# Query features of the three kept token blocks: turned by VectorE in pieces of 32 rows and put together in DRAM, in place of TensorE transposes with ScalarE copies

## The chip, the cores and the metric

The kernel runs on one core of a Trainium2 chip. A core has five engines that run their own instruction streams: TensorE (PE in the profile, with its weight loads as PEld), VectorE (DVE), ScalarE (ACT), GpSimd (POOL) and SyncE (SP), whose queue issues nearly all DMA transfers here. Sixteen DMA engines move the data. The metric is the device time of one execution in microseconds (us); lower is better.

## The reference

Four layers, alternately A and B, act on x of 2048 tokens by 576 features, all in float32. A is attention of 32 heads of 18 with one shared key and value head. B is linear attention with learned feature maps, and the change lies in B:

```python
phi_q = concat([softmax(q @ w_phi), softmax(-(q @ w_phi))])   # per head: 18 + 18 = 36 features
phi_k = concat([softmax(k @ w_phi), softmax(-(k @ w_phi))])
kv = einsum("bhsf,bhsd->bhfd", phi_k, v);  z = einsum("bhsf->bhf", phi_k)
o  = einsum("bhqf,bhfd->bhqd", phi_q, kv) / (einsum("bhqf,bhf->bhq", phi_q, z) + 1e-6)
x  = x + o.reshape(B, S, D) @ wo        # x is layer-normed before q, k, v
```

The sum over all tokens in kv and z means that no output of B can be made before the keys of the last token are in. The query features of a token (32 heads x 36 = 1152 numbers) can be made earlier, and have to be kept until then.

## The kernel before, in words

The tokens are cut into 16 blocks of 128. The program runs over two layers (`LAYERS = 2`), each one A followed by one B.

*The attention of A* (`attend`) runs block by block in bursts of scores, exponentials on ScalarE and sums. Between the bursts TensorE also does the work of B for blocks whose attention is done: `mix` projects keys, values and queries of a block, adds the keys to the state `kv`, and turns the query features, which lie as tokens x features, into features x tokens. This it does with `block_transpose`: one VectorE instruction turns each 32 x 32 square of the 128 x 1152 tile in place of its square, and four DMAs, one for each 32 tokens, put the squares where they belong in a DRAM tensor, `spill[i]` of 1152 x 128. One such DMA moves 32 features x 36 squares x 32 tokens; a contiguous piece is 32 numbers, 128 bytes.

*The end of the layer.* The last three blocks, `KEPT = 13`, 14 and 15, are done after the attention, in `leave`. There `keys_in` makes the keys and the state (`first_keys`, `second_keys`, `last_keys`) and `queries_in` the query features: `queries` (two halves of 28 matmuls on `wpq`, in the weight place c, each followed by `feature_start`, VectorE and an exponential on ScalarE), `feature_end` for both halves (a sum and a reciprocal on VectorE, the multiply on GpSimd), then `flip_features` and `spill_features`. `flip_features` turns the 1152 features in 11 groups of 108 (the last of 72) by TensorE against an identity, four groups to a PSUM bank, and ScalarE copies them to the tile `phs` (L676, L681). `spill_features` writes it with two DMAs in pieces of 512 bytes (L693, L694). The features of block 13 live in the tile `featk`, those of block 14 in `featq`, those of block 15 in the room `xsc`. The tile `phs` has two buffers. In `leave` TensorE's instructions are chained in the order in which they were traced.

`leave` also fetches weights again: `wob` into place a and, in layer 0, `wq` into place b (L220). `finish_state` lays the state out as `kvb`, and with that the read-out can begin.

*The read-out of B* (`token_tile`, 16 jobs): the features of a block come back from DRAM (`load_features`, L698 and L699, tile `pht`, one buffer for even and one for odd blocks), `read_out` multiplies them with `kvb` (44 matmuls, L804), divides by the sums on VectorE (L811 to L814), turns the result by TensorE (L307, L311), splits it into a high and a low part (ScalarE L132, L313, VectorE L135, L316), projects with `wob` (2 x 14 matmuls, L257) and adds the residual (L321). In layer 0 `next_queries` and `project_queries` follow, which begin the next attention; in layer 1 the block is written to the output.

*The order.* `pipelined` advances the jobs in rounds. In each round one more job starts, and each started job runs to its next `yield STAGE`; then the late jobs get their turn, among them `flips(leave())`. `leave()` runs whole before the first round. When it returns, block 13 is done, block 15 has both halves of its projection, block 14 only the first. `flips` does the rest in spread-out rounds: after one round the second half of block 14's projection; three rounds later its `feature_end`, transposes and spill; two rounds later those of block 15. `advance(job, n)` counts negative yields, which stand for TensorE work. The rounds give the order of tracing; a scheduler then sets the order on each engine, earlier traced work first where it is ready by its own estimate of times. The SP queue and each engine work in the order so fixed, and an instruction that waits holds up those behind it.

Of the kernel before, what the change touches and what calls it, by code (L numbers as in the profile page):

```python
# [62 lines left out]
def kernel(ctx, tc, x_in, wq, wk, wv, wo, wqkv, w_phi, wob, out):  # L63
# [209 lines left out]
    def run(gen):  # L273
        for _ in gen:
            pass
# [390 lines left out]
                feature_end(e, 0, V)  # L666
            yield from project(po, st["wpq"], b * HALF, xs, lambda: feature_start(heads(po), e, b, copies))

    def flip_features(e, pht, ps, copies):
        phi = e.rearrange("p h s d -> p (h s d)")  # L670
        for g0 in (0, 4, 8):
            g1 = min(g0 + 4, NKG)
            pt = ps.tile([P, 4, P], F32, name="ps")
            for g in range(g0, g1):
                m = 2 * DH * (KG if g < NKG - 1 else H - KG * (NKG - 1))
                T.transpose(pt[:m, g - g0, :], phi[:, g * 6 * DH : g * 6 * DH + m], idf)  # L676
            g2 = min(g1, NKG - 1)
            parts = [(slice(0, 6 * DH), g0, g2)] + ([(slice(0, 4 * DH), NKG - 1, NKG)] if g1 == NKG else [])
            for rows, ga, gb in parts:
                if copies is A:  # L680
                    A.activation(pht[rows, ga:gb, :], pt[rows, ga - g0 : gb - g0, :], AF.Copy)  # L681
                else:
                    V.tensor_copy(pht[rows, ga:gb, :], pt[rows, ga - g0 : gb - g0, :])
            yield -440
        return pht

    def feature_rows(spill, i):
        full = 6 * DH * (NKG - 1)
        return (spill[i, :full, :].rearrange("(g r) t -> r g t", r=6 * DH), spill[i, full:, :])

    def spill_features(pht, spill, i):
        rows, rest = feature_rows(spill, i)
        nc.sync.dma_start(rows, pht[: 6 * DH, : NKG - 1, :])  # L693
        nc.sync.dma_start(rest, pht[: 4 * DH, NKG - 1, :])  # L694

    def load_features(pht, spill, i):
        rows, rest = feature_rows(spill, i)
# [3 lines left out]
    def block_transpose(blocks, src, dst, pause=0):  # L701
        V.transpose(blocks, src)
        for _ in range(pause):
            yield
        for q in range(P // 32):
            rows = slice(q * 32, (q + 1) * 32)
            nc.sync.dma_start(dst[:, rows].rearrange("(b f) t -> f b t", f=32),
                              blocks[rows, :].rearrange("f (b t) -> f b t", t=32))
            yield
# [41 lines left out]
    def queries_in(i, xs, eq, st, ps, spill):  # L751
        yield from queries(xs, eq, st, ps, A)
        for b in range(2):
            feature_end(eq, b, G)
        pht = st["sp"].tile([P, NKG, P], F32, name="phs", bufs=2)
        yield from flip_features(eq, pht, ps, A)
        spill_features(pht, spill, i)

    def advance(job, count=1):
        while count:  # L760
            v = next(job, DONE)
            if v is DONE:
                return
            count -= v is not STAGE and not isinstance(v, Kind) and v < 0
# [514 lines left out]
    for layer in range(LAYERS):  # L1279
# [194 lines left out]
        with psx, tc.tile_pool(name=f"s{layer + 1}", bufs=2) as sp:  # L1474
            if not last:
                reload_w4(sp)

            def leave():
                xn = layer_norm(c, stats, sp, A, "xo")
                advance(second_keys)  # L1480
                xl = sp.tile([P, 9, P], F32R, name="xs3")
                advance(transposed(xn, xl, ps, A, LOE), 2)
                queued = [queries_in(i, x, feature_room(name), st, ps, spills[layer])
                          for i, x, name in ((KEPT, kept, "featk"), (c - 1, xs, "featq"))]
                advance(queued[0])
                both = sp.tile([P, 9, PW], F32R, name="xsc").bitcast(F32).rearrange("p a b -> p (a b)")
                ek, eq = (both[:, k * 2 * D : (k + 1) * 2 * D].rearrange("p (h s d) -> p h s d", s=2, d=DH)
                          for k in range(2))
                last_keys = keys_in(c, xl, ek, st, ps)
                queued.append(queries_in(c, xl, eq, st, ps, spills[layer]))  # L1490
                advance(last_keys, 2)
                run(load("wob", "a", wob, slice(0, D), engines=(A, V)))
                advance(last_keys, 2)
                if not last:
                    run(load("wq", "b", wq, slice(0, D), engines=(A, G)))
                advance(queued[0])
                advance(last_keys)
                advance(queued[2])
                run(finish_state(st, sp, ps))
                advance(queued[2])  # L1500
                advance(queued[1])
                run(queued[0])
                before = None
                for i in traced(nc)[mark:]:
                    if i.engine == mybir.EngineType.PE:
                        if before is not None:
                            tc.add_manual_dep(i, before, NOSYNC, reason="order")
                        before = i.name
                return queued[1:]

            def flips(queued):
                for rounds, job, count in ((1, 0, 1), (3, 0, 3), (2, 1, 3)):
                    for _ in range(rounds):
                        yield STAGE
                    advance(queued[job], count)
                for job in queued:
                    run(job)

            def room(i):
                if i % 2:  # L1520
                    return sp.tile([P, NKG, P], F32, name="pht", bufs=1)
                return bw.tile([P, NKG, P], F32, name="pht")

            def token_tile(i):
                pht = room(i)
                load_features(pht, spills[layer], i)
                if i not in left:
                    xres[i] = sp.tile([P, D], F32, name="xt", bufs=6)
                    nc.sync.dma_start(xres[i], xd[i])
                yield STAGE  # L1530
                yield STAGE
                yield from read_out(i, pht, st, sp, ps)
                if last:
                    nc.sync.dma_start(out[i * P : (i + 1) * P, :], xres[i])
                else:
                    nc.sync.dma_start(xd[i], xres[i])
                    yield STAGE
                    yield from next_queries(i, None, layer + 1, st, bw, sp, ps)

            order = range(NT)  # L1540
            st["sp"] = sp
            jobs = [token_tile(i) for i in order]
            for job in jobs[:2]:
                next(job)
            st["late"].append(flips(leave()))
            if last:
                run(pipelined(jobs, st["late"]))
            else:
                settle(layer + 1, ps, jobs)
# [27 lines left out]
```

## Time and profile before

| | |
|---|---|
| three runs | 2676.86, 2673.14, 2677.76 us (median 2676.86) |
| the profiled execution | 2676.42 us, span of the trace 2674.6 us |
| mean granted TensorE clock | 0.991 |
| L676: transposes of the three blocks, TensorE | 66 in the run, 33 in each layer |
| L681: their copies, ScalarE | 24 in the run, 9.1 us |
| L693, L694: their spills, SP | 6 + 6 issues |
| L702 on `pht<-featq`: the same turn for the other 13 blocks, VectorE | 26 in the run, 35.8 us |
| L707 on `phi<-pht`: their spills, SP | 104 issues |

The end of layer 0 (from the last scores of its attention to the first of the next) lies at about 1216 to 1452 us of the span, that of layer 1 at 2525 to 2675. Times in the profile's rows are from the span's start. A row of the instructions in order of time reads: start us, length us, engine, line, operation, output<-input, shapes, count, and in brackets the idle time of the engine before it with what ended that. A row of stretches reads: start:end, length, then busy us of PE, PEld, DVE, ACT and POOL, each with its number of instructions, the granted TensorE clock, the mean busy share of the 16 DMA engines, and GB/s. A row of groups ends with busy us, mean ns of one, and idle time before them with its causes. SPq is SP's queue: the time there is that of issuing. TensorE's matmuls overlap, so the lengths of neighbouring rows can sum to more than the time between their starts.

### The profile page before, as it was taken

The page shows a single profiled execution, that of the slowest core. Times are in us where ns is not written, and L with a number is a line of the kernel's source. Part 1 is how long each engine was busy: PE and PEld are TensorE (multiplying, and loading weights), DVE is VectorE, ACT ScalarE, POOL GpSimd, SP SyncE. Part 2 cuts the span into 40 slices and gives each one's busy share as a digit, 9 for nine tenths or more (in the row PEclk, how much of TensorE's full clock was granted, in tenths as well). Part 3 has the DMA queues.
Part 4 walks back from the last instruction along what each step waited for, and adds up shares of the span by engine and source line. Part 5 has one row for each costly group of instructions (what it writes and reads, how often), then busy time and mean ns, then how long its engine had stood idle before and what let it go on. Part 6 is the DMA issues. An engine that isn't in the chain of part 4 may idle for free. (4 is left out here: it accounts for less than half of the span.)

```text
span 2674.6 us, 55524 instructions
## 1 busy us (share of the span) xinstructions
PE 2602.2 (97%) x22002; PEld 1442.2 (54%) x22002; DVE 1265.0 (47%) x2871; ACT 2153.8 (81%) x2529; POOL 66.0 (2%) x106
## 2 busy tenths in 40 slices
PE   7989999999999999999999999999999999999999
PEld 6633454445444444438996344444444444444498
DVE  8435354444444444436774424444444444444265
ACT  4588889989999999994334999999999999999821
POOL 1000000000000000002000000000000000000010
PEclk9999999999999999999999999999999999999999
DMA  5466243222222222225643312222222222222164
GB/s 182 144 146 171 70 127 100 59 53 60 60 59 57 55 57 57 59 66 158 188 152 105 105 51 59 60 60 60 59 60 59 60 60 57 56 55 55 48 196 140
DMA packets 491634, 232.97 MB, mean 87 GB/s; under 512 B 237734, under 2 KB 458214, under 8 KB 491366
## 3 DMA queue, kind: packets, MB, share of 16 engines
q1 hardware_dynamic: 489894, 226.37, 31.4%
q8 instruction: 177, 2.90, 0.5%
q10 hardware_dynamic: 1472, 2.95, 0.4%
q14 instruction: 91, 0.75, 0.1%
HBM read 130.62 MB, written 96.67 MB: 85 GB/s over the span
## 5 line engine op out<-in xcount | busy, mean ns | idle before, releaser
L1047 ACT ACTIVATE pt<-sc 128x1024 f32<-128x1024 f32 x2036 | 1923.4, 1054 | 180.4 <-PE sc L574 160.3
L574 PE MATMUL sc<-qst,kst 56*128 56x512 f32 x3840 | 698.6, 452 | 21.0 <-ACT pt L1047 20.6
L574 PEld LDWEIGHTS sc<-qst,kst 56*128 56x128 f32 x3840 | 319.4, 185 | 561.7 <-ACT pt L1047 511.8
L853 PE MATMUL acc<-pt,vst 128*32 128x512 f32 x4096 | 499.8, 600 | 0.1
L853 PE MATMUL ps<-pt,vst 128*32 128x512 f32 x4048 | 486.7, 604 | 6.1 <-DVE featq L607 3.2
L853 PEld LDWEIGHTS ps<-pt,vst 128*32 128x32 f32 x4048 | 109.8, 110 | 234.0 <-issue 226.1
L853 PEld LDWEIGHTS acc<-pt,vst 128*32 128x32 f32 x4096 | 104.6, 109 | 211.7 <-issue 209.2
L321 DVE TENSOR_TENSOR xc<-xc,acc 128x288 f32<-128x288 f32 x60 | 27.3, 455 | 349.5 <-PE acc L257 349.5
L257 PE MATMUL ps<-wahi,xs 128*128 128x288 f32 x702 | 152.5, 304 | 2.5 <-ACT xs L132 1.9
L257 PE MATMUL ps<-wchi,xs 128*128 128x288 f32 x576 | 127.2, 307 | 0.0
L257 PE MATMUL acc<-wdhi,on 128*128 128x288 f32 x540 | 120.6, 309 | 3.3 <-DMA on<-od 3.3
L257 PEld LDWEIGHTS ps<-wahi,xs 128*128 128x128 f32 x702 | 116.1, 190 | 7.1 <-ACT xs L132 2.6
L257 PE MATMUL ps<-walo,xs 128*128 128x288 f32 x390 | 114.9, 297 | 0.0
L452 PE MATMUL ps<-xsc,wbhi 128*128 128x256 f32 x576 | 107.3, 285 | 0.6 <-ACT xsc L132 0.6
L474 ACT ACTIVATE pc<-ps 128x256 fp32r<-128x256 f32 x80 | 30.4, 384 | 94.0 <-PE ps L452 92.5
L257 PEld LDWEIGHTS ps<-wchi,xs 128*128 128x128 f32 x576 | 94.1, 188 | 19.0 <-issue 18.1
L607 DVE COPY featk<-acc 128x288 f32<-128x288 f32 x50 | 22.8, 457 | 172.0 <-PE acc L257 172.0
L132 ACT ACTIVATE xs<-ps 128x512 fp32r<-128x512 f32 x36 | 21.4, 595 | 102.6 <-PE ps L307 102.6
L257 PEld LDWEIGHTS acc<-wdhi,on 128*128 128x128 f32 x540 | 88.8, 189 | 25.0 <-issue 23.6
L257 PE MATMUL acc<-wahi,xs 128*128 128x288 f32 x450 | 100.0, 308 | 0.5
L257 PE MATMUL ps<-wclo,xs 128*128 128x288 f32 x320 | 94.3, 295 | 0.0
L452 PEld LDWEIGHTS ps<-xsc,wbhi 128*128 128x128 f32 x576 | 91.2, 192 | 1.6 <-ACT xsc L132 1.1
(261 smaller groups left out, 3062.3 us busy)
## 6 DMA issues: line engine op xcount, KB each, us to landing
qst<-qd SPq DMA_DIRECT2D x360, 72.0 KB
od<-parts SPq DMA_DIRECT2D x512, 36.0 KB
pht<-phi SPq DMA_DIRECT2D x32, 540.0 KB
qd<-pc SPq DMA_DIRECT2D x64, 256.0 KB
on<-od SPq DMA_DIRECT2D x60, 256.0 KB
phi<-pht SPq DMA_DIRECT2D x104, 144.0 KB
xd<-xc SPq DMA_DIRECT2D x33, 288.0 KB
flipped<-pht SPq DMA_DIRECT2D x112, 72.0 KB
```

The costliest lines, as they stand in the source:

```text
L132: A.activation(dst_hi, src, AF.Copy)
L257: T.matmul(dst, xs[:, slot, :], w[half][:, k, c0 : c0 + HALF], start=(n == 0), stop=(n == last))
L321: V.tensor_add(xr, xr, po)
L452: T.matmul(po, lhs, xsc[:, slot, :], start=(n == 0), stop=(n == LASTP))
L474: A.activation(pc[:, 0, :], po, AF.Copy)
L574: T.matmul(sc, kst[head_rows(h), t * P : (t + 1) * P], q[head_rows(h), h // 2, :], start=True, stop=True)
L607: V.tensor_copy(e[:, hs, 0, :], src)
L853: T.matmul(acc[32 * j : 32 * j + 32, :], vst[:, t, :], pts[j], start=first, stop=last)
L1047: A.activation(pt, sc, AF.Exp, scale=SCALE)
```

## The change

`queries_in` takes the way of the other blocks: after `feature_end` one VectorE instruction turns the 128 x 1152 features square by square into a tile of the tag `phs` (128 x 1152 in place of 128 x 11 x 128, still two buffers), and four DMAs write it to the same DRAM tensor in the same layout. `load_features` and all that reads are as before. `flip_features` and `spill_features` go. `flips` waits one round and then runs block 14 to its end (second half of the projection, `feature_end`, turn, spill) and block 15 after it. In `leave`, block 13 runs to its end at the same place as before.

```diff
-    def flip_features(e, pht, ps, copies):
-        phi = e.rearrange("p h s d -> p (h s d)")
-        for g0 in (0, 4, 8):
-            g1 = min(g0 + 4, NKG)
-            pt = ps.tile([P, 4, P], F32, name="ps")
-            for g in range(g0, g1):
-                m = 2 * DH * (KG if g < NKG - 1 else H - KG * (NKG - 1))
-                T.transpose(pt[:m, g - g0, :], phi[:, g * 6 * DH : g * 6 * DH + m], idf)
...
-                    A.activation(pht[rows, ga:gb, :], pt[rows, ga - g0 : gb - g0, :], AF.Copy)
...
-            yield -440
-        return pht
...
-    def spill_features(pht, spill, i):
-        rows, rest = feature_rows(spill, i)
-        nc.sync.dma_start(rows, pht[: 6 * DH, : NKG - 1, :])
-        nc.sync.dma_start(rest, pht[: 4 * DH, NKG - 1, :])
...
         yield from queries(xs, eq, st, ps, A)
         for b in range(2):
             feature_end(eq, b, G)
-        pht = st["sp"].tile([P, NKG, P], F32, name="phs", bufs=2)
-        yield from flip_features(eq, pht, ps, A)
-        spill_features(pht, spill, i)
+        blocks = st["sp"].tile([P, 2 * D], F32, name="phs", bufs=2)
+        run(block_transpose(blocks, eq.rearrange("p h s d -> p (h s d)"), spill[i]))
+        yield STAGE
...
             def flips(queued):
-                for rounds, job, count in ((1, 0, 1), (3, 0, 3), (2, 1, 3)):
-                    for _ in range(rounds):
-                        yield STAGE
-                    advance(queued[job], count)
+                yield STAGE
                 for job in queued:
                     run(job)
```

The function that it now calls, unchanged:

```python
def block_transpose(blocks, src, dst, pause=0):
    V.transpose(blocks, src)
    for _ in range(pause):
        yield
    for q in range(P // 32):
        rows = slice(q * 32, (q + 1) * 32)
        nc.sync.dma_start(dst[:, rows].rearrange("(b f) t -> f b t", f=32),
                          blocks[rows, :].rearrange("f (b t) -> f b t", t=32))
        yield
```

More of the change, by code (lines that the diff above doesn't have):

```diff
@@ L667, in queries @@
             yield from project(po, st["wpq"], b * HALF, xs, lambda: feature_start(heads(po), e, b, copies))
-    def flip_features(e, pht, ps, copies):
-        phi = e.rearrange("p h s d -> p (h s d)")
-        for g0 in (0, 4, 8):
-            g1 = min(g0 + 4, NKG)
-            pt = ps.tile([P, 4, P], F32, name="ps")
-            for g in range(g0, g1):
-                m = 2 * DH * (KG if g < NKG - 1 else H - KG * (NKG - 1))
[L676 to L683, printed above, removed]
-            yield -440
-        return pht
     def feature_rows(spill, i):
```

## The prediction

> **What bounds the kernel now.** I read the page first, then the work by stretches, then the chain of waits and the instructions in order of time around the removed lines. The first line below is the page's share of engines. The next two are stretches: the ends of the two layers, where the changed code runs (start:end, length, busy us of each engine with its instructions, TensorE clock, DMA share, GB/s).
>
> ```profile
> PE 2602.2 (97%) x22002; PEld 1442.2 (54%) x22002; DVE 1265.0 (47%) x2871; ACT 2153.8 (81%) x2529; POOL 66.0 (2%) x106
> ...
> 1216.00:1452.00 236.00, 229.83 (x2481) 219.26 (x2473) 170.86 (x513) 80.42 (x187) 25.17 (x34) 0.99 0.54 166
> 2525.00:2675.00 150.00, 144.12 (x1775) 137.23 (x1769) 93.79 (x267) 31.09 (x72) 15.07 (x14) 0.99 0.50 154
> ```
>
> In these stretches PE is busy 97% and 96% of the time, ScalarE (ACT) 34% and 21%. So a microsecond taken from PE counts, one taken from ScalarE hardly does, and VectorE (72% and 63%) is next. In the chain that ended last, the removed transposes of layer 1 stand as three pieces (start, us):
>
> ```profile
> 2568.37 1.20 PE ps L676 x11
> ...
> 2586.53 1.34 PE ps L676 x11
> ...
> 2595.75 1.34 PE ps L676 x11
> ```
>
> Together 3.88 us. For layer 0 I take the distance from each group's start to the next PE work, from the instructions in order of time:
>
> ```profile
> 1258.80 1.36 PE L676 MATMUL ps<-idf,featk 128*108 128x128 f32 x11
> 1260.23 1.48 PE L804 MATMUL ps<-kvb,pht 108*64 108x57 f32 x44
> ...
> 1280.19 1.15 PEld L676 LDWEIGHTS ps<-idf,featq 128*108 128x108 f32 x11
> ...
> 1281.34 0.47 PEld L307 LDWEIGHTS ps<-idf,xn 128*128 128x128 f32 x4
> ...
> 1290.69 1.15 PEld L676 LDWEIGHTS ps<-idf,xsc 128*108 128x108 f32 x11
> ...
> 1291.83 0.19 PEld L257 LDWEIGHTS ps<-wahi,xs 128*128 128x128 f32 x1
> ```
>
> That is 1.43 + 1.15 + 1.14 = 3.72 us. The whole prize is 3.88 + 3.72 = 7.60 us, 0.28% of the run, if nothing else ends later.
>
> But one place of layer 0 is not bound by PE. Token tile 2 waits for its features from DRAM; the rows are PE's first read-out of tile 2 with the idle time before it, the SyncE (SP) queue ahead of that load, and stretches around it:
>
> ```profile
> 1262.32 1.54 SPq L220 DMA_DIRECT2D wblo<-wqd  x1
> 1263.97 0.34 SPq L693 DMA_DIRECT2D phi<-phs  x1
> 1264.40 1.99 SPq L694 DMA_DIRECT2D phi<-phs  x1
> 1266.49 0.85 SPq L698 DMA_DIRECT2D pht<-phi  x1
> 1267.39 2.59 SPq L699 DMA_DIRECT2D pht<-phi  x1
> ...
> 1273.69 0.29 PE L804 MATMUL ps<-kvb,pht 108*64 108x57 f32 x2 [1.55 <-DMA pht<-phi]
> ...
> 1272.00:1274.00 2.00, 0.45 (x5) 0.28 (x3) 1.94 (x8) 0.00 (x0) 0.84 (x1) 0.97 0.77 217
> 1274.00:1276.00 2.00, 2.00 (x9) 2.00 (x9) 1.26 (x2) 0.00 (x0) 1.95 (x3) 0.50 0.64 189
> 1276.00:1278.00 2.00, 2.00 (x12) 2.00 (x12) 0.77 (x2) 1.12 (x2) 0.00 (x0) 0.68 0.10 15
> ...
> 1262.00:1272.00 10.00, 9.06 (x100) 8.35 (x98) 9.19 (x26) 2.32 (x5) 2.33 (x2) 1.00 0.93 301
> 2572.00:2582.00 10.00, 9.06 (x106) 8.22 (x104) 9.02 (x27) 2.32 (x5) 3.50 (x3) 1.00 0.63 191
> ```
>
> The DMA engines are 93% busy there (reload of wq, then the spill of block 13, then tile 2's features), so the load's landing at 1273.7 is set by what lies ahead of it in the queue, and PE idles 1.55 us. The stall also costs speed: the granted clock is 0.97, 0.50 and 0.68 in three 2-us stretches, which is 2 x (0.03 + 0.50 + 0.32) = 1.7 us of full-speed PE. In layer 1 the DMA share at the same point is 0.63 and no such wait stands.
>
> The rule of the Trainium skill, page "TensorE: Matmul & The Clock Gate", part "The HAM clock gate", is that the clock halves after an idle window of about 3.4 us and recovers after as long a busy one. The trace shows the halving after a shorter idle time, so by the row any stall of 1.5 us may cost another 1.7 us, by the rule only one that fills a window; the sum below needs neither, since this stall stays and no new one is forecast.
>
> **The change part by part.** Removed in each layer: 33 transposes on PE (3.72 and 3.88 us) and 12 copies on ScalarE. PE waited for those copies only this much in the whole run (us, times; from the groups of the read-out's weight loads):
>
> ```profile
> L804 PEld LDWEIGHTS ps<-kvb,pht 108*64 108x64 f32 (+1 forms) x1408 | 44.1, 138 | 7.4 <-issue 6.1 <-ACT phs L681 0.5 <-PE ps L307 0.3
> ```
>
> These 0.5 us lie inside the distances above. Otherwise the copies count as nothing: ScalarE's idle time in these stages hides them.
>
> Added: six VectorE transposes and 24 DMA issues in place of 12. Both are in the trace, because the other 13 blocks of each layer go that way already (groups of instructions; issues with shortest/median/longest ns; a spill of the attention stage, the last thing issued before the stretch that follows; POOL's second multiply of block 13):
>
> ```profile
> L702 DVE STREAM_TRANSPOSE pht<-featq 128x1152 f32<-128x1152 f32 x26 | 35.8, 1377 | 0.8
> ...
> L707 SPq DMA_DIRECT2D phi<-pht x104: 307/587/1825, 343.1 to 2477.2; - x104
> ...
> 1166.13 2.54 SPq L707 DMA_DIRECT2D phi<-pht  x3
> ...
> 1168.00:1170.00 2.00, 1.58 (x14) 0.57 (x16) 0.00 (x0) 2.00 (x4) 0.00 (x0) 1.00 1.15 190
> ...
> 2566.42 1.17 POOL L621 TENSOR_TENSOR featk<-featk,fz 128x576 f32<-128x576 f32 x1 [4.11 <-DVE fz L620]
> ```
>
> VectorE gets 3 x 1.377 = 4.13 us per layer. The spill keeps its 1152 x 128 x 4 = 589,824 bytes, but in 4608 pieces of 128 bytes rather than 1152 of 512. At 190 GB/s it fills the engines for 589,824 / 190e3 = 3.1 us, against 589,824 / 301e3 = 2.0 us at the mixed rate of 1262 to 1272: 1.1 us more each. On SP four issues of 0.59 us make 2.3 us, as L693 and L694 took (0.34 + 1.99); at the longest, 1.8 each, 7.3 us.
>
> Waits that are new: a VectorE transpose stands behind POOL's second multiply of its block (1.17 us), the third also behind the landing of block 13's spill, whose buffer it takes (two buffers). What is queued behind it on VectorE are the splits and divisions of the token tiles (L135, L811 to L814) and the residual adds (L321), and PE's projections (L257) wait for those splits. On SP, the loads of the next tiles' features and residuals queue behind the spills. Moved: all features of blocks 14 and 15 are traced in the second round rather than up to the seventh, so their reductions, multiplies and spills come forward, into 1266 to 1280 and 2575 to 2588.
>
> *Layer 1.* PE gains 3.88. VectorE has this much room and these waits (its busy time is in the third number after the length):
>
> ```profile
> 2568.00:2570.00 2.00, 1.98 (x28) 1.75 (x28) 1.78 (x5) 1.75 (x4) 0.00 (x0) 1.00 0.21 22
> 2570.00:2572.00 2.00, 2.00 (x44) 1.95 (x41) 1.26 (x7) 0.92 (x3) 0.00 (x0) 1.00 0.40 102
> ...
> 2580.67 0.69 DVE L135 TENSOR_TENSOR xs<-ps,xs 128x512 fp32r<-128x512 f32 x1 [0.41 <-ACT xs L132]
> ...
> 2583.80 0.46 DVE L321 TENSOR_TENSOR xt<-xt,ps 128x288 f32<-128x288 f32 x1 [0.94 <-PE ps L257]
> ```
>
> From 2568 to 2582 its idle time is 0.22 + 0.74 + 0.98 = 1.94 us (the last from 9.02 busy in ten). So 4.13 - 1.94 = 2.2 us of its work runs late at 2582, just where tile 1's split (2580.67) is what PE waits for; after 2583.8 it idles again and catches up. Between 0 (the order puts the transposes behind the splits) and 4.13 (all exposed) I take 2.2. The spill's extra DMA time I cost at 0 here, covered by the free 37% of the DMA engines (3.7 us in those ten); without that cover it is 1.1. Layer 1: -3.88 + 2.2 = -1.7.
>
> *Layer 0.* The first group's 1.43 us is gained ahead of the wait for tile 2, so it only lengthens that wait: 0. The load of tile 2 now stands behind a spill that takes 1.1 us longer: +1.1 (between 0, if the spill gets ahead of the wq reload, which VectorE's earlier finish allows, and 5.0, SP's 7.3 less 2.3). The other two groups come after the wait: -1.15 - 1.14 = -2.29. VectorE's extra 4.13 us I cost at 0: PE waits for the DMA until about 1274.8 whatever VectorE does, and the added work ends by then; without that cover it costs up to 2.2 as in layer 1. Layer 0: -1.2.
>
> Sum: -1.7 - 1.2 = -2.9. The profiled execution took 2676.42 us around its span of 2674.6, 0.4 under the median of the three runs (2676.86), so no correction is due: **2673.5 us**. About 0.2% (5.4 us) is what a measurement of this kernel can tell from no change, and this is less.
>
> **The rivals.**
> - *All of it hidden (0.22).* VectorE's transposes fall in its gaps and tile 2's features land no later: -3.88 - 2.29 - 1.43 = -7.6, 2668.8. For it: the DMA falls to 0.10 busy at 1276, VectorE is idle again after 2583. Against: VectorE is 92% and 90% busy just where the work is put.
> - *VectorE becomes the bound (0.20).* Its transposes, traced ahead of the tiles' splits, are taken first in both layers: 2 x 4.13 of exposed time and 1.1 of DMA against 7.6: +1.8, 2678.2. For it: PE already waits at 2580.69 for one split. Against: in layer 0 PE waits for a DMA then.
> - *The loads queue behind the spills: slower (0.10).* All three spills of a layer get onto SP ahead of tile 2's features: 3 x 3.1 instead of 2.0, so these land 7.3 us later. Layer 0: 7.3 - 2.29 = +5.0. Layer 1: the load was issued by 2574.2 (below); with the 3.7 us that it took from issue to use in layer 0 (1269.98 to 1273.69) it lands at 2577.9, then at 2585.2. PE wants it at 2581.4 less 1.2: 5.0 us of stall and 1.7 of clock against 3.88: +2.8. Together +7.8, 2684.2. It decides from about 6 us of lateness in both layers. For it: SP is first come, first served and the spills are now traced before tile 2's load. Against: that load is free to go as soon as tile 0 is read out, before block 14's second half is even projected.
>
> ```profile
> 2573.28 0.92 SPq L699 DMA_DIRECT2D pht<-phi  x1
> ...
> 2581.41 0.56 PE L804 MATMUL ps<-kvb,pht 108*64 108x57 f32 x10
> ```
>
> The Trainium skill speaks for this rival: "DMA: Bandwidth & Descriptors", section Specifications, asks for pieces of at least 512 bytes, and "VectorE: DVE Perf Modes", section "Rules for kernel authors", sends a 128 x 128 transpose to TensorE. By the first, the trace agrees (190 against 301 GB/s); no row here shows the second.
> - *The change does not do what it says (0.03).* PE's freed slots refill with waits one for one: 2676.4.
>
> **How the numbers follow.** The forecast has 0.45; its own range is 2670.2 (VectorE's and the spill's costs at 0) to 2675.5 (VectorE's at 4.13). Faster by over 0.2%: the hidden case and the lower edge of the forecast, 0.22 + 0.05 = 0.27. Slower: the queue rival and the upper edge of the VectorE one, 0.10 + 0.02 = 0.12. Within: 0.61. The range 2667.5 to 2681 takes in the hidden case and the VectorE one and leaves out most of the queue rival.
>
> **What would show it.** Right: no L676 or L681; L702 on phs six times at 1.38 us; PE's wait for tile 2's features in layer 0 above 3 us, landing near 1275; in layer 1 a PE wait of 1 to 2 us on an L135 split; the end of layer 0 earlier by about 1 us and of layer 1 by about 2 more. Wrong: tile 2's load landing before 1273 in layer 0 (the hidden case), PE waits on splits above 3 us in both layers (VectorE), or waits on pht in layer 1 and for tile 3 (the queue).

## The result

The change made the kernel slower: 2703.98 us median of five runs (2702.12 to 2709.11) against 2674.34 for the kernel before beside it, ratio 1.0110, 95% interval 1.0096 to 1.0125. That is 30 us worse, outside the predicted range (2667.5 to 2681), and on the side of the rival "the loads queue behind the spills", though almost four times as dear as that rival was priced (+7.8).

The profiled execution of the changed kernel took 2703.98 us with a span of 2702.2, 27.6 more than before. To see where they lie I cut both traces at the same instructions: the first copy to `osb` after a layer's attention opens the end of a layer, the first exponential of the next attention (on `wchi`) closes that of layer 0, and the last residual add closes that of layer 1. In the trace of before these stand at 1216.91, 1449.21, 2526.24 and 2671.01; in that of the changed kernel (instructions in order of time) here:

```profile
1214.98 0.60 ACT L885 ACTIVATE osb<-acc 128x512 f32<-128x512 f32 x1 [1.20 <-PE acc L830]
...
1461.26 1.94 ACT L1024 ACTIVATE wchi<-sc 128x1024 f32<-128x1024 f32 x2 [2.85 <-PE sc L574]
...
2538.72 0.60 ACT L885 ACTIVATE osb<-acc 128x512 f32<-128x512 f32 x1 [1.20 <-PE acc L830]
...
2698.31 0.46 DVE L321 TENSOR_TENSOR xc<-xc,ps 128x288 f32<-128x288 f32 x1 [1.14 <-PE ps L257]
```

The end of layer 0 grew from 232.30 to 246.28 us (+13.98), that of layer 1 from 144.77 to 159.59 (+14.82); the attention between them from 1077.03 to 1077.46. So both ends lost about the same. All experiments below are read by these two lengths, since the first mark itself varied from 1210.7 to 1217.6 between profiled runs. Each length is that of one execution. The attention between the two ends, which no run changes, varied from 1075.3 to 1078.8, so a difference of a us or two between two ends may be chance.

The page's engine line and the stretches of the two ends after the change:

```profile
PE 2605.3 (96%) x21936; PEld 1442.9 (53%) x21936; DVE 1272.1 (47%) x2877; ACT 2145.5 (79%) x2505; POOL 66.0 (2%) x106
...
1214.00:1464.00 250.00, 229.54 (x2448) 218.46 (x2440) 174.28 (x516) 76.19 (x175) 25.21 (x34) 0.96 0.53 157
2537.00:2702.00 165.00, 147.48 (x1746) 139.59 (x1738) 97.48 (x270) 27.18 (x60) 15.03 (x14) 0.94 0.49 140
```

TensorE is busy 92% and 89% of the two ends (97% and 96% before), at a clock of 0.96 and 0.94 instead of 0.99: the 66 transposes are gone, and its busy time has still risen by 3.1 us, because it ran slower. VectorE has 3.4 and 3.7 us more.

SP's queue and TensorE's idle times in layer 0 after the change show where:

```profile
1260.94 24.55 SPq L684 DMA_DIRECT2D phi<-phs  x12
1285.59 0.94 SPq L675 DMA_DIRECT2D pht<-phi  x1
...
1258.31 1.48 PE L781 MATMUL ps<-kvb,pht 108*64 108x57 f32 x44 [1.26 <-DMA kvb<-featx]
1270.88 0.64 PE L307 MATMUL ps<-idf,xo 128*128 128x128 f32 x4 [2.50 <-DVE xo L790]
1272.27 0.61 PE L257 MATMUL ps<-wahi,xs 128*128 128x288 f32 x1 [0.27 <-ACT xs L132]
1291.72 2.58 PE L781 MATMUL ps<-kvb,pht 108*64 108x57 f32 x44 [12.82 <-DMA pht<-phi]
```

All twelve spill issues of blocks 13, 14 and 15 (L684) stand on SP ahead of tile 2's load (L675). They occupy the queue for 24.55 us, and the load goes at 1285.59, 70.6 us after the first mark, instead of 1266.49, 49.6 after it. TensorE waits 12.82 us for it (1.55 before). What SP itself waited for in that time (us, times, longest), and the last of VectorE's three turns:

```profile
SPq L684 <- DVE phs L679: 10.3, 1, 10.3
...
SPq L684 <- DVE fz L620: 2.6, 1, 2.6
...
1281.15 1.38 DVE L679 STREAM_TRANSPOSE phs<-xsc 128x1152 f32<-128x1152 f32 x1
```

The third turn, block 15's, starts at 1281.15, though the block's features were multiplied by about 1270.8 (GpSimd's last multiply of `xsc` started at 1269.62 and took 1.16). On VectorE it stands behind the residual adds and statistics of tile 1. No idle time stands right before it, and from 1269 to 1270 the DMA share is down to 0.02 with block 13's spill moved, so by 1281 it is its place in VectorE's order, and no longer its buffer, that makes it late. Ten of the 24.55 us are SP waiting for it, and for most of them the DMA engines have nothing to do. The stretches show that, and the clock:

```profile
1268.00:1271.00 3.00, 0.50 (x4) 0.30 (x4) 2.97 (x9) 0.00 (x0) 2.19 (x2) 1.00 0.54 77
1271.00:1278.00 7.00, 6.70 (x29) 6.18 (x29) 4.03 (x12) 1.89 (x4) 0.54 (x1) 0.53 0.48 71
1278.00:1282.00 4.00, 0.90 (x6) 0.66 (x5) 2.29 (x6) 0.00 (x0) 0.54 (x1) 0.93 0.00 0
1282.00:1291.00 9.00, 0.00 (x0) 0.00 (x0) 0.53 (x1) 0.00 (x0) 0.00 (x0) 0.50 0.72 140
1291.00:1296.00 5.00, 4.28 (x54) 4.08 (x54) 1.87 (x7) 0.62 (x2) 0.00 (x0) 0.57 0.71 232
```

From 1278 to 1282 the DMA share is 0.00; then block 15's spill and the late loads move, with TensorE idle. The granted clock is 0.53 in the seven us after the wait of 2.50 and 0.57 in the five after the wait for tile 2: 7 x 0.47 + (5 x 0.43 less half of the 0.72 us still idle) = 5.1 us of full-speed TensorE, 3.4 more than the 1.7 of before. With the waits (1.26 + 2.50 + 0.27 + 12.82 = 16.85, against 0.31 + 0.64 + 1.55 = 2.50 in the same stretch before) that is 14.35 - 3.72 + 3.4 = 14.0, the 13.98 measured.

Layer 1 after the change (SP's queue, SP's waits, TensorE's idle times, VectorE around the two parts of tile 1's split, stretches):

```profile
2581.41 21.77 SPq L684 DMA_DIRECT2D phi<-phs  x12
2603.29 1.15 SPq L675 DMA_DIRECT2D pht<-phi  x1
...
SPq L684 <- DVE fz L620: 9.9, 1, 9.9
...
2582.84 1.48 PE L781 MATMUL ps<-kvb,pht 108*64 108x57 f32 x44 [2.08 <-DMA kvb<-featx]
...
2594.76 0.37 PE L257 MATMUL ps<-wahi,xs 128*128 128x288 f32 x1 [2.02 <-issue]
...
2610.08 2.58 PE L781 MATMUL ps<-kvb,pht 108*64 108x57 f32 x44 [6.12 <-DMA pht<-phi]
...
2589.12 0.63 DVE L135 TENSOR_TENSOR xs<-ps,xs 128x512 fp32r<-128x512 f32 x1
...
2592.72 1.38 DVE L679 STREAM_TRANSPOSE phs<-featq 128x1152 f32<-128x1152 f32 x1 [0.53 <-POOL featq L621]
2594.36 0.29 DVE L316 TENSOR_TENSOR xs<-ps,xs 64x128 fp32r<-64x128 f32 x1
...
2596.00:2604.00 8.00, 7.36 (x33) 6.75 (x33) 3.79 (x9) 0.77 (x2) 0.00 (x0) 0.59 0.72 106
2604.00:2608.00 4.00, 0.00 (x0) 0.00 (x0) 0.45 (x1) 0.00 (x0) 0.00 (x0) 0.75 0.87 193
2608.00:2616.00 8.00, 5.28 (x75) 4.68 (x77) 2.69 (x9) 0.77 (x2) 0.00 (x0) 0.50 0.73 208
```

The same order on SP, with the load 64.6 us after the mark instead of 46.7; here SP's long wait (9.9) falls on block 14, whose second half is only projected after tile 0's read-out. A second loss is VectorE's: between the two parts of tile 1's split (L135 at 2589.12, L316 at 2594.36) stand block 14's and 15's sums and block 14's turn, and TensorE, which needs the split, starts 0.4 us after its second part does, having waited 2.02 us. The granted clock is then 0.59 and, behind the wait for tile 2, 0.50. Layer 0 has the like: the 2.50 us before 1270.88 are a wait for tile 1's division, which stands on VectorE behind the sums of blocks 14 and 15 and block 14's turn.

### The profile page after: what moved, and what is told of

It is laid out like the page before. It is cut to its first block, busy times and chain, and to the rows that moved or that the text cites. A ratio compares the mean times of both kernels' runs of the same rounds, so it can differ in the third digit from the quotient of the medians.

```text
span 2702.2 us, 55360 instructions
## 1 busy us (share of the span) xinstructions
PE 2605.3 (96%) x21936; PEld 1442.9 (53%) x21936; DVE 1272.1 (47%) x2877; ACT 2145.5 (79%) x2505; POOL 66.0 (2%) x106
```

## The experiments

My theory after these traces: the 29 us are a matter of order. `flips` now traces blocks 14 and 15 whole in its second round, so their spills stand on SP ahead of tile 2's load, and that load waits for features that don't exist yet. Rivals: the pieces of 128 bytes; the turns on VectorE; the missing third buffer of `phs`. The table has the lengths of the two ends in the profiled runs less those of before (232.30 and 144.77), and the ratio of the medians to the kernel before beside them.

| kernel | end of layer 0 | end of layer 1 | ratio (95%) |
|---|---|---|---|
| the change | +13.98 | +14.82 | 1.0110 (1.0096 to 1.0125) |
| three buffers of `phs` | +5.84 | +14.18 | 1.0075 (1.0056 to 1.0094) |
| long pieces | +4.05 | +9.42 | 1.0060 (1.0041 to 1.0079) |
| spills on ScalarE's queue | +3.66 | +10.74 | 1.0062 (1.0045 to 1.0078) |
| three buffers, spills of 14 and 15 later | +2.36 | +6.23 | 1.0034 (1.0020 to 1.0048) |
| rounds as before | +2.50 | +0.49 | 1.0019 (1.0008 to 1.0029) |
| rounds as before, long pieces | +0.58 | +1.77 | 1.0005 (0.9995 to 1.0016) |
| rounds as before, block 15's turn moved | -1.69 | +0.99 | 0.9996 (0.9986 to 1.0005) |
| that, and the state's transposes earlier | -1.89 | -1.18 | 0.9999 (0.9990 to 1.0008) |
| rounds, turn moved, block 13 by TensorE | +0.88 | -1.54 | 1.0000 (0.9991 to 1.0009) |
| rounds, turn moved, a half of block 14 in `leave` | +1.04 | +6.32 | 1.0013 (1.0002 to 1.0025) |
| kernel before with the new `flips` | +5.36 | +8.83 | 1.0058 (1.0041 to 1.0076) |

**Rounds as before.**

```diff
-                yield STAGE
-                for job in queued:
-                    run(job)
+                for rounds, job, count in ((1, 0, 1), (3, 0, 0), (2, 1, 0)):
+                    for _ in range(rounds):
+                        yield STAGE
+                    if count:
+                        advance(queued[job], count)
+                    else:
+                        run(queued[job])
```

> The changed kernel with one thing put back: `flips` spreads its work over rounds as before (after one round the second half of block 14's projection, three rounds later block 14's turn and spill, two later block 15's). The turns by VectorE and the spills in 128-byte pieces stay. Only block 13's four spill issues then stand on SP ahead of tile 2's load; those of block 14 stand behind tile 4's. Theory (the order on SP costs the time): nearly all of the 14.0 us of layer 0 and the 14.8 us of layer 1 goes, and 2668 to 2677 us is left, ratio to the kernel before 0.997 to 1.001. Rival (128-byte pieces are what costs, about 4 us a spill against 2): the same bytes move in the same pieces, so at least 2 us a spill, 12 us in all, stays: 2685 or more. Rival (VectorE's six turns and the waits they put ahead of the tiles' splits): the turns stay, 2685 or more.

Measured: 2677.67 us beside 2672.13, ratio 1.0019. SP in layer 0:

```profile
1260.89 6.30 SPq L684 DMA_DIRECT2D phi<-phs  x4
1267.29 0.75 SPq L675 DMA_DIRECT2D pht<-phi  x1
```

Four issues stand ahead of tile 2's load instead of twelve, and it goes 18 us sooner. 11.5 of 14.0 us and 14.3 of 14.8 go, with every turn and every short piece still in place: both those rivals are out as the main cause. By its ratio the kernel stays above the forecast (0.997 to 1.001), so the turns and spills did not bring the gain they were meant to; the later runs look for it.

**Three buffers of `phs`**, the change otherwise as it is.

```diff
-        blocks = st["sp"].tile([P, 2 * D], F32, name="phs", bufs=2)
+        blocks = st["sp"].tile([P, 2 * D], F32, name="phs", bufs=3)
```

> The changed kernel with three buffers of `phs` in place of two, so that block 15's turn doesn't have to wait for the landing of block 13's spill. The order on SP is the same as in the changed kernel (12 spill issues ahead of tile 2's load); on VectorE block 15's turn stands some 20 instructions earlier. Theory: in layer 0 the turn comes at about 1272 instead of 1281, SP's wait of 10.3 us shrinks to about 2, tile 2's load is issued about 8 us earlier, and 8 to 9 of the 14 us go; in layer 1 the turn was late by 3.3 us, so about 3 of the 14.8 go: 2690 to 2695 us, ratio 1.006 to 1.008. Rival (the missing buffer is the whole cause): 2680 or less. Rival (pieces or bandwidth): no change, 2702 to 2706.

Measured: 2694.39, ratio 1.0075. Layer 0 gave back 8.1 of 14.0, as worked out; layer 1 only 0.6 of 14.8 (3 were expected). SP's queue and TensorE's wait, layer 0, then SP in layer 1:

```profile
1259.87 16.06 SPq L684 DMA_DIRECT2D phi<-phs  x12
...
1282.71 1.90 PE L781 MATMUL ps<-kvb,pht 108*64 108x57 f32 x44 [4.28 <-DMA pht<-phi]
...
2572.05 23.15 SPq L684 DMA_DIRECT2D phi<-phs  x12
```

The third turn now comes at 1269.75 and the twelve issues take 16 us instead of 24.55. In layer 1 they still take 23: there the queue waits for block 14's features, which no buffer makes sooner. The missing buffer is the larger part of layer 0's loss and nearly none of layer 1's. It costs by the order: with three buffers the third turn is built in at an earlier place on VectorE.

**Spills of blocks 14 and 15 later**, with three buffers.

```diff
+        turn = block_transpose(blocks, eq.rearrange("p h s d -> p (h s d)"), spill[i], 1)
+        next(turn)                      # the turn alone
+        later.append(turn)              # its four DMAs
...
+                run(later.pop())        # in leave: block 13's DMAs, as before
...
                 yield STAGE
                 for job in queued:
                     run(job)
+                for rounds in (3, 2):
+                    for _ in range(rounds):
+                        yield STAGE
+                    run(later.pop(0))
```

> The changed kernel with three buffers of `phs`, and with the spills of blocks 14 and 15 alone moved back: their projection, sums, multiplies and turns stay in the second round, and their eight issues are traced three and five rounds later. VectorE's order is that of the run with three buffers but for a few small neighbours; SP has only block 13's four issues ahead of tile 2's load. Theory (the order on SP): in both layers the wait on pht goes, and the end of layer 1, which three buffers left 14.2 us longer than before, comes down to within 3 us of before: 2674 to 2681 us in all, ratio 1.000 to 1.003. Rival (the early projections and turns themselves, which push the tiles' divisions and splits back on VectorE): layer 1 stays 8 us or more longer, 2684 or more.

Measured: 2683.12, ratio 1.0034, between the two forecasts. Only eight DMA issues per layer have moved against the run with three buffers, and the ends fall by another 3.5 and 8.0 us; no wait of TensorE on `pht` over 0.3 us is left at tile 2. So in layer 1 SP's order is worth 8 of the 14.8 us. But 6.2 us stay there, which I had given to the rival only from 8 on. They are VectorE's:

```profile
2575.46 0.62 DVE L135 TENSOR_TENSOR xs<-ps,xs 128x512 fp32r<-128x512 f32 x1
2576.03 0.75 DVE L619 TENSOR_REDUCE fz<-featq 128x32 f32<-128x576 f32 x1
2576.70 0.74 DVE L619 TENSOR_REDUCE fz<-xsc 128x32 f32<-128x576 f32 x1
...
2579.04 1.38 DVE L679 STREAM_TRANSPOSE phs<-featq 128x1152 f32<-128x1152 f32 x1 [0.52 <-POOL featq L621]
...
2580.69 0.29 DVE L316 TENSOR_TENSOR xs<-ps,xs 64x128 fp32r<-64x128 f32 x1
...
2581.08 0.37 PE L257 MATMUL ps<-wahi,xs 128*128 128x288 f32 x1 [2.01 <-issue]
2583.96 1.09 PE L307 MATMUL ps<-idf,xo 128*128 128x128 f32 x4 [2.10 <-DVE den L791]
```

Some 4.6 us of block 14's and 15's work, 1.38 of it the turn and 0.52 a wait for GpSimd, stand between the two halves of one split, and TensorE waits for the second. With the rounds as before this work spreads out and those 6 us go too.

**The kernel before with the new `flips`** (TensorE's transposes, no turn, no short piece).

```diff
-                for rounds, job, count in ((1, 0, 1), (3, 0, 3), (2, 1, 3)):
-                    for _ in range(rounds):
-                        yield STAGE
-                    advance(queued[job], count)
+                yield STAGE
                 for job in queued:
                     run(job)
```

> The kernel before (TensorE transposes, ScalarE copies, two spill issues of 512-byte pieces) with only `flips` changed: block 14 and 15 run to their ends in the second round. All six spill issues of a layer then stand on SP ahead of tile 2's load. Theory (the order on SP): slower than the kernel before, as the load waits for block 15's features, though less than by 27 us, since the copies of block 15 don't wait for a buffer as long and a spill takes 2 us: 2682 to 2698, ratio 1.003 to 1.009, with waits of TensorE on pht in both layers. Rivals (pieces; VectorE's turns): neither is in this kernel, so 2673 to 2677.

Measured: 2689.32, ratio 1.0058, in the forecast band, but not by the mechanism forecast. Tile 2's load stands behind block 13's spill alone (at 1264.61), blocks 14's and 15's spills behind it and ahead of tile 3's. What TensorE waits for, in layer 0:

```profile
1264.33 0.76 PE L676 MATMUL ps<-idf,featq 128*108 128x128 f32 x5 [2.58 <-POOL featq L621]
1267.50 1.52 PE L676 MATMUL ps<-idf,featq 128*108 128x128 f32 x6 [2.41 <-POOL featq L621]
```

That is 5.0 us, and layer 1 has the same two waits (2.58 and 2.40): TensorE's own transposes now come up in its queue before GpSimd has multiplied the features. So with the same `flips` SP's order was built another way here; which spills stand ahead of a load can be read from the built program, not from the diff. So the move of `flips` costs by itself, in either version; which queue pays depends on the version, TensorE here, SP and VectorE in the change.

**Spills on ScalarE's queue**, the change otherwise as it is.

```diff
-            nc.sync.dma_start(dst[:, rows].rearrange("(b f) t -> f b t", f=32),
+            (queue or nc.sync).dma_start(dst[:, rows].rearrange("(b f) t -> f b t", f=32),
...
-        run(block_transpose(blocks, eq.rearrange("p h s d -> p (h s d)"), spill[i]))
+        run(block_transpose(blocks, eq.rearrange("p h s d -> p (h s d)"), spill[i], queue=nc.scalar))
```

> The changed kernel with the 12 spill issues of the kept blocks in each layer on ScalarE's queue instead of SP's; the turns, pieces, bytes and `flips` stay as changed. Tile 2's and 3's loads then stand on SP behind no spill. Theory (head of line on SP): the load of tile 2 goes at about 1266 in layer 0 and 2573 in layer 1, and the two PE waits of 12.8 and 6.1 us go; ScalarE's own work behind the waiting issues (the tiles' copies L132 and L313) may stall instead, so 2672 to 2688, ratio 0.999 to 1.005. Rival (the DMA engines' time for 128-byte pieces): the loads share the engines with the same pieces and land as late: 2698 or more. Rival (VectorE): the turns stand as they were, 2690 or more.

Measured: 2688.12, ratio 1.0062, just above the forecast (up to 2688, ratio 1.005). No wait of TensorE on `pht` at tile 2 is left, though the same short pieces share the same engines. But the stall has gone to the queue that issues now, here in layer 1:

```profile
2579.90 17.04 ACTq L684 DMA_DIRECT2D phi<-phs  x8
2597.04 0.60 ACT L132 ACTIVATE xs<-ps 128x512 fp32r<-128x512 f32 x1 [19.97 <-DMA phi<-phs]
...
2597.69 0.40 PE L257 MATMUL ps<-wahi,xs 128*128 128x288 f32 x1 [3.48 <-ACT xs L132]
```

ScalarE does no arithmetic for 19.97 us; its copy for a tile stands behind eight waiting issues, and TensorE waits 3.48 us for that copy. In layer 0 it waits 4.05 us for one behind block 13's issues. So this part of the loss follows the issues from one queue to the other. Another 3.22 us of waiting in layer 1, before 2580.70, is for VectorE's part of a split, behind the early sums and block 14's turn, which this run leaves as they were.

**Long pieces**, with `flips` as changed and with the rounds as before. The features of blocks 13 to 15 land in another order, so their read-out isn't the reference's; the bytes are the same.

```diff
-            nc.sync.dma_start(dst[:, rows].rearrange("(b f) t -> f b t", f=32), ...)
+            nc.sync.dma_start(spill[i].rearrange("(p a) t -> p (a t)", p=P)[rows, :], blocks[rows, :])
```

> The changed kernel, `flips` as changed, two buffers, with each spill DMA writing 32 pieces of 4608 bytes instead of 1152 of 128 (the same bytes; the features of blocks 13 to 15 land in the order of the tokens, so their read-out multiplies other numbers than the reference's). The built order puts block 15's turn where three buffers put it, so the run to compare with is the one with three buffers (2694.39, ratio 1.0075): same turns, same order on SP in layer 0, only the pieces differ. Theory (SP waits for features that aren't made yet, not for the transfer): SP is done 1 to 2 us sooner in layer 0 and in layer 1 about as much, so 2 to 4 us less than with three buffers: ratio 1.006 to 1.007. Rival (the slow pieces are the price, about 4 us a spill against less than 2): 6 us or more less in layer 0 alone, ratio 1.005 or below.

> The changed kernel with the rounds of `flips` as before (the kernel that came to 2677.67), and with each of the four spill DMAs writing 32 pieces of 4608 bytes instead of 1152 of 128. The same bytes move; the features of blocks 13, 14 and 15 land in the order of the tokens, so the read-out of these three blocks multiplies other numbers than the reference's. Theory: with the order put back the pieces are not on the path; TensorE's waits left there are on kvb (1.69 and 1.34 us) and on xo (3.93 and 2.16), not on pht: 2675 to 2680, within 0.1% of the kernel with rounds and short pieces. Rival (short pieces still cost 1 to 2 us each through the loads that share the engines): 2670 to 2674.

Measured: 2688.07, ratio 1.0060, and 2676.62, ratio 1.0005. In layer 0, where turns and SP's order equal those of the run with three buffers, the long pieces gave 1.8 us (+5.84 to +4.05), and TensorE's wait for tile 2 fell from 4.28 to 2.90: at most a small part, though 1.8 us between two single executions is hardly clear of chance. In layer 1 (4.8) they can't be read alone, since block 14's spill there no longer stands ahead of tile 2's load. With the rounds as before the two intervals (1.0008 to 1.0029 with short pieces, 0.9995 to 1.0016 with long) overlap, so a cost of up to some 4 us is neither shown nor excluded there. What the pieces cost the DMA engines is plainer, in stretches in which SP has only spills under way (128 bytes in the changed kernel; 512 in the kernel before with the new `flips`; 4608 in the changed kernel with long pieces):

```profile
1272.00:1274.00 2.00, 1.73 (x8) 1.73 (x8) 1.80 (x5) 0.39 (x2) 0.00 (x0) 0.50 1.00 149
```

```profile
2588.00:2590.00 2.00, 2.00 (x33) 1.67 (x34) 0.50 (x1) 1.31 (x4) 0.00 (x0) 0.65 0.81 232
```

```profile
1270.00:1272.00 2.00, 1.07 (x5) 0.60 (x5) 1.91 (x7) 0.64 (x2) 0.54 (x1) 0.79 0.98 258
```

A spill of 589,824 bytes is 4.0 us at 149 GB/s, 2.5 at 232 and 2.3 at 258.

**Block 15's turn behind tile 2's division**, rounds as before. With rounds as before TensorE's longest waits left are these (layer 0, layer 1):

```profile
1258.53 1.48 PE L781 MATMUL ps<-kvb,pht 108*64 108x57 f32 x44 [1.69 <-DMA kvb<-featx]
...
1280.25 1.07 PE L307 MATMUL ps<-idf,xo 128*128 128x128 f32 x4 [3.93 <-DVE xo L790]
...
2570.04 1.48 PE L781 MATMUL ps<-kvb,pht 108*64 108x57 f32 x44 [1.34 <-DMA kvb<-featx]
...
2589.43 0.78 PE L307 MATMUL ps<-idf,xo 128*128 128x128 f32 x4 [2.16 <-DVE xo L790]
```

```diff
+                    tc.add_manual_dep(turn, st["xos"][-3], NOSYNC, reason="order")   # tile 2's last copy into xo
```

> The kernel with the rounds of `flips` as before (2677.67), with one instruction moved: block 15's turn on VectorE is made to stand behind the division of tile 2 (the last copy into its xo) instead of right before it; SP's order is the same. If the turn's place on VectorE is what left that kernel 5 us behind, TensorE's waits of 3.93 us (layer 0) and 2.16 us (layer 1) on xo shrink by the turn's 1.3 us and by the wait ahead of it, to under 1.5 together: 2671 to 2674, ratio 0.999 to 1.0005. If it isn't, 2676 to 2679.

Measured: 2673.58, ratio 0.9996: level with the kernel before. The waits on xo are 1.46 and 0.93 instead of 3.93 and 2.16, together 2.39, above the 1.5 forecast; the time is in the forecast. The end of layer 0 is 4.2 us shorter, that of layer 1 0.5 longer. One instruction's place on VectorE held most of what the rounds had left.

**What swallowed the rest.** Three runs on top of that one. The state's transposes earlier, so that `kvb` lands sooner:

```diff
                 advance(last_keys)
-                advance(queued[2])
+                for _ in range(4):
+                    next(queued[2])
                 run(finish_state(st, sp, ps))
+                advance(queued[2])
```

> The kernel with rounds as before and block 15's turn behind tile 2's division (2673.58), with the transposes of the state (`finish_state`) traced after 6 of the 14 products of block 15's first half instead of after all 14, so about 1.0 us earlier on TensorE (8 products of 0.135 us). Theory: TensorE's wait for kvb, 1.26 us in layer 0 and 1.46 in layer 1, is what swallowed the gain of block 13's removed transposes; about 1.0 us of it goes in each layer, unless the transposes of the state now wait for VectorE's last addition to it: 2671 to 2673, ratio 0.998 to 0.9995. If that wait takes its place, no change.

Measured: 2671.26, ratio 0.9999, above the forecast 0.998 to 0.9995. The waits for `kvb` are 0.47 and 0.82 instead of 1.26 and 1.46, and in the profiled run the two ends together are 3.1 us shorter than without the move; the medians don't show it. Block 13 by TensorE as before, the other two by VectorE (`if i == KEPT:` with the old `flip_features` and `spill_features`):

> The kernel with rounds as before and block 15's turn behind tile 2's division (2673.58), with block 13 turned by TensorE again (11 transposes, three ScalarE copies, two spill issues of 512-byte pieces); blocks 14 and 15 stay with VectorE. Theory: the 1.2 to 1.4 us of TensorE that block 13's group takes in each layer lie under the wait for kvb (1.26 and 1.46 us), which then shows in no row; so the time is that of the kernel without them, 2672 to 2675, and removing this group was worth nothing. Rival (the group was on the path, as the prediction had it for layer 1): 1 to 3 us slower, 2675 to 2677.

Measured: 2671.97, ratio 1.0000. No wait for `kvb` is left in either layer; the 11 transposes stand in its place. The ratio differs from the run without them by 0.04%, less than either interval is wide. The profiled ends go opposite ways (+2.6 and -2.5 against that run). So it is as the theory has it within what can be told: that group covered a wait. And the second half of block 14's projection moved ahead of the first read-out, in place of the state's move:

```diff
-                advance(queued[1])
+                advance(queued[1], 2)
```

> As the run before in this call (block 15's turn behind tile 2's division), with the second half of block 14's projection moved from the second round into `leave`, ahead of the first read-out. The removed transposes of block 13 stood just ahead of that read-out and covered the landing of kvb; without them TensorE waits 1.69 and 1.34 us for it. The 28 matmuls cover that: 2 to 3 us less than the run before, 2668 to 2672, ratio 0.998 to 0.9995. Rival (these matmuls are then missing where they covered the division of tile 0): a wait on xo of 1 to 3 us in each layer, no gain or slower, 2672 to 2679.

Measured: 2679.71, ratio 1.0013: the rival, and just above its 2679. The wait for `kvb` goes, and TensorE waits 2.10 us in each layer for the division of tile 0, which those matmuls had covered, 2.48 instead of 1.46 for that of tile 2 in layer 0, and 2.07 for a later tile's features in layer 1. No version is faster than the kernel before by more than the measurement can tell.

## Why the prediction was wrong

*The step that failed* is the argument against the queue rival: "that load is free to go as soon as tile 0 is read out, before block 14's second half is even projected". The load was free, but SP took what stood first: the order was fixed when the program was built, with all twelve issues ahead, and they held the queue for 24.55 and 21.77 us. So the sum's term for that load, +1.1 in layer 0 and 0 in layer 1, was far too small: TensorE waited 12.82 and 6.12 us. I had quoted the very sentence ("first come, first served and the spills are now traced before tile 2's load") and given it 0.10. What is ready first was a guess about the scheduler. Tracing order alone would not have settled it either: with the same `flips`, SP's order came out otherwise with TensorE's transposes, and in layer 1 with long pieces. What decides is the built order: with a third buffer and the spills of blocks 14 and 15 later, 11.6 and 8.6 of the 13.98 and 14.82 us go.

*The rival's own price failed too*: "7.3 us later". It counted three transfers at 3.1 us. The load came 21.0 us later after the mark in layer 0 and 17.9 in layer 1, because the queue spent most of that time waiting for features: 14.0 us in layer 0 (10.3 for block 15's turn) and 14.1 in layer 1 (9.9 until the reciprocals of block 14's sums). The prediction did name the third turn's wait "for the landing of block 13's spill" and what stands behind it on VectorE, but not that SP would stand behind the turn. With three buffers, which give that turn an earlier place, 8.1 us of layer 0's loss go.

*"VectorE's extra 4.13 us I cost at 0" in layer 0, "2.2" in layer 1.* With SP's order mended, 6.2 us stay in layer 1 from the early work and, with the rounds as before, one turn's place costs 4.2 us in layer 0. In the changed kernel, too, TensorE waits 2.50 us in layer 0 behind that work. The turn's length was right (1.38 each); what costs is its place: it, the sums and the waits for GpSimd stand ahead of splits and divisions that TensorE waits for. That VectorE "idles again and catches up" after 2583.8 did not help: TensorE had waited 2.02 us for the split by then, and the granted clock was 0.59 in the eight us that followed.

*The prize of 7.60 us* was counted whole in layer 1 and less the first 1.43 in layer 0. Block 13's 11 transposes stood ahead of the wait for `kvb` in both layers. Without them TensorE waits 1.26 and 2.08 us there, a wait that no row of the kernel before could show, but that I could have looked for in the inputs of the instruction just behind the removed ones. So the prize was at most about 5 us (7.60 less 1.43 and 1.20).

*The spill* was sized at "3.1 us" by a row of mixed traffic (190 GB/s); a spill by itself runs at 149 GB/s, 4.0 us. The spill of before, sized at "2.0" by another mixed row, takes 2.5 by itself, so the short pieces cost about 1.4 us a spill against the "1.1" of the sum. Nor did four issues make "2.3 us" on SP: with the order mended block 13's held it 6.30 us in layer 0 and 2.90 in layer 1. It matters little: the long pieces gave 1.8 us in layer 0.

*The clock*: "no new one is forecast". The waits cost 5.1 us of full-speed TensorE in layer 0, 3.4 more than before. The Trainium skill, page "TensorE: Matmul & The Clock Gate", part "The HAM clock gate", adds that its window of about 3.4 us runs free of what the kernel does. No trace here shows the window itself. After a wait of 2.50 us that ended at 1270.88 the clock was 1.00 up to 1271 and 0.53 from then to 1278, so here a wait shorter than that window was followed by half clock, and only after it was over.

*Right*: L676 and its copies gone, six turns of 1.38 us, a wait on tile 1's split in layer 1 (2.02 us), and the sign of the queue rival: "waits on pht in layer 1" was named and is there, 6.12 us, though none stands at tile 3.

## What to carry to other kernels

When a change moves work earlier in the trace, write down for each in-order queue, the DMA-issuing ones first, what then stands ahead of the next load that somebody waits for, as the built program has it, and when the last of it can be ready. An issue that waits for data costs its wait on top of its transfer (here 10.3 us for one against 4.0 for a whole spill). A stretch removed just ahead of a wait is worth only what that wait leaves of it, and the next instruction's inputs tell. Two changes in one edit (here the turn and the rounds of `flips`) are best priced apart: with the rounds as before the turn was worth about nothing, and the new rounds cost 26 of the 29 us with VectorE's turns, 14 with TensorE's.

## What the runs showed of the hardware

- SBUF to DRAM in pieces of 128 bytes ran at 149 GB/s at a DMA share of 1.00, the same bytes in pieces of 512 at 232 at 0.81, in pieces of 4608 at 258 at 0.98 (each in a stretch of two us).
- A wait of 2.50 us on TensorE in the changed kernel was followed by a granted clock of 0.53 for seven us, in which TensorE was busy for 6.70.
- DMA issues on ScalarE's queue that waited held up ScalarE's own arithmetic: 8 issues took 17.04 us, and ScalarE computed nothing in the 19.97 us before the copy behind them.
